# Scores on sixteen 32x32 tiles: x turned by VectorE in blocks, fixed PSUM banks, one x buffer

## The chip, the cores and the metric

One core of one Trainium2 chip. The metric is the device time in microseconds (us); the median of several executions is quoted. TensorE (PE in the profile) multiplies matrices into PSUM, a memory of eight banks of 128 x 512 fp32. VectorE (DVE), ScalarE (ACT) and GpSimd (POOL) work element by element, SyncE (SP) issues most DMA transfers. Ratios are the mean time of one kernel's fast runs over that of the other's fast runs of the same rounds, so they are not quite the ratio of the medians quoted.

## The reference

Eight batches of tokens (512 tokens, 8 heads of 64) attend to 32 state vectors per head, and the states attend to the tokens. A feed-forward layer with ELU follows.

```python
B, H, S, Ns, D = (8, 8, 512, 32, 64)
scores  = scale * x @ state.T          # softmax over the 32 states
xread   = softmax(scores) @ state
scores2 = scale * state @ x.T          # softmax over the 512 tokens
sread   = softmax(scores2) @ x
# rows of both, 8 x 544 tokens of 512, go through
h = rows @ w_in                        # 512 -> 2048
g = where(h > 0, h, exp(min(h, 0)) - 1)
out = g @ w_out                        # 2048 -> 512
```

x and state are random with a deviation of 0.1. Scores are therefore around 0.01, the softmax is nearly even, and a mistake in the scores hardly shows in the output.

## The kernel before

Both softmaxes come from one product, scores with states on partitions and tokens along the row. For it TensorE turns x, ACT copies the turned x out of PSUM, and TensorE multiplies on eight 64x32 tiles. `banks` hands out the one two-bank tile that all these steps share.

```python
xpool = pool("x", 2)
ps_a = pool("ps_a", 1, space=PSUM)     # 2 banks: turns, scores, m, state read
ps_h = pool("ps_h", 3, space=PSUM)     # hidden layer
ps_o = pool("ps_o", 3, space=PSUM)     # outputs

def turn_x(b, i):                      # 8 turns of 128x128; called twice a batch
    ps = banks([P, 2, R, P], "xT_ps")
    for j in range(2):
        for r in range(R):
            m = 2 * i + j
            transpose(ps[:, j, r], x_t[b][:, r, m * P : (m + 1) * P])

def by_state(b, name, rhs):            # scores, and m = states x w_in
    ps = banks([P, G, 512], name)
    for m in range(NP):
        for g in range(G):
            d = slice(g * D, (g + 1) * D)
            matmul(ps[m * NS : (m + 1) * NS, g], kT[d, b, m * NS : (m + 1) * NS],
                   rhs[m][d], start=True, stop=True, tile_position=(g * D, m * NS))
    return ps
# ... softmaxes on VectorE, ACT and GpSimd; state read; m ...
def ffn1(b, fo):                       # one of 16 parts of the hidden layer
    ps = ps_h.tile([P, S], FP32, tag="h", name="h_ps")
# ...
steps = [lambda i=i: (turn_x(b, i), copy_x(b, i)) for i in range(2)]
return steps + [s0, nop, nop, s1, lambda: (state_read(b), keep_read(b))]
```

After each hidden layer come two halves of a second product by Strassen's scheme (`p1` to `p7`: seven products of 16 instructions each, 3.46 us). The attention of the next batch is cut into the steps of the last line, and one step goes behind each product. In the first batch the order is a fixed plan, mixed with the conversion of the weights from fp64.

Of the kernel before, what the change touches and what calls it, by code (L numbers as in the profile page):

```python
# [10 lines left out]
FP32 = mybir.dt.float32  # L11
# [14 lines left out]
def kernel(  # L26
# [17 lines left out]
    DM, DF = moe_w_in.shape  # L44
    P = 128
    R = S // P
    NP = H // 2
    G = 2
    FO = DF // P
# [16 lines left out]
        return ctx.enter_context(tc.tile_pool(name=name, bufs=bufs, **kw))  # L66

    cpool = pool("const", 1)
    xpool = pool("x", 2)
    apool = pool("attn", 2)  # L70
    atpool = pool("aT", 4)
    mpool = pool("m", 2)
    work = pool("work", NRAW + 4)
    small = pool("small", 4)
    epool = pool("elu", 3)
    opool = pool("o", 2)
    ps_a = pool("ps_a", 1, space=PSUM)
    ps_h = pool("ps_h", 3, space=PSUM)
    ps_o = pool("ps_o", 3, space=PSUM)

    def banks(shape, name):
        return ps_a.tile(shape, FP32, tag="a", name=name)



# [48 lines left out]
        return raw  # L134

    def turn_states(raw):
        ps = st["k_ps"] = banks([P, B, P], "k_ps")
        for b in range(B):
            transpose(ps[:, b], raw[:, b].rearrange("p c d -> p (c d)"))

# [52 lines left out]

    def turn_x(b, i):

        ps = banks([P, 2, R, P], "xT_ps")
        for j in range(2):
            for r in range(R):
                m = 2 * i + j
                transpose(ps[:, j, r], x_t[b][:, r, m * P : (m + 1) * P])  # L200
        st[b, "xT", i] = ps
# [6 lines left out]
                out=xT[:, j], in_=st[b, "xT", i][:, j].rearrange("p r q -> p (r q)")  # L208
            )

    def by_state(b, name, rhs):


        ps = banks([P, G, 512], name)
        for m in range(NP):
            for g in range(G):
                d = slice(g * D, (g + 1) * D)
                matmul(
                    ps[m * NS : (m + 1) * NS, g],
                    kT[d, b, m * NS : (m + 1) * NS],  # L220
                    rhs[m][d],
                    start=True,
                    stop=True,
                    tile_position=(g * D, m * NS),
                )
        return ps

    def scores(b):

        st[b, "s_ps"] = by_state(b, "s_ps", [st[b, m] for m in range(NP)])  # L230



    def column_max(b, g):
        st[b, g, "top"] = top = small.tile([P, 1], FP32, name="top")
        vector.reduce_max(top, st[b, "s_ps"][:, g], axis=AX_X)
        vector.tensor_scalar(
            out=top, in0=top, scalar1=-scale, scalar2=None, op0=ALU.mult
        )

    def turn_scores(b, g):
        st[b, g, "t"] = t = apool.tile([P, NB, NS], FP32, name="t_sb")
        vector.transpose(t.rearrange("p k n -> p (k n)"), st[b, "s_ps"][:, g])

    def column_exp(b, g):
        st[b, g, "total"] = small.tile([P, 1], FP32, name="total")
        st[b, g, "a_s"] = apool.tile([P, S], FP32, name="a_s")
        scalar.activation(
            out=st[b, g, "a_s"], in_=st[b, "s_ps"][:, g], func=AF.Exp, scale=scale,
            bias=st[b, g, "top"], accum_out=st[b, g, "total"],  # L250
        )

# [33 lines left out]
        vector.transpose(st[b, g, "aT"], st[b, g, "t"].rearrange("p k n -> p (k n)"))  # L286

    def turn_state(b):
        ps = st[b, "sT"] = banks([P, G, R, P], "sT_ps")
        for g in range(G):  # L290
            a = st[b, g, "a_s"].rearrange("p (r q) -> p r q", r=R)
            for r in range(R):
                transpose(ps[:, g, r], a[:, r])
# [6 lines left out]
    def state_read(b):  # L300


        ps = st[b, "sr"] = banks([P, G, 512], "sr_ps")
        for g in range(G):
            for r in range(R):
                for m in range(NP):
                    matmul(
                        ps[m * NS : (m + 1) * NS, g, :D],
                        st[b, "aT_s"][:, g, r, m * NS : (m + 1) * NS],
                        x_t[b][:, r, m * P + g * D : m * P + (g + 1) * D],  # L310
                        start=(r == 0),
                        stop=(r == R - 1),
                        tile_position=(0, m * NS),
                    )
# [7 lines left out]

    def turn_read():

        ps = banks([P, B, NP, NS], "rT_ps")
        for b in range(B):
            transpose(ps[:, b].rearrange("p m s -> p (m s)"), read[:, b].rearrange("p g d -> p (g d)"))
        st["xT"] = work.tile([P, NP, B, NS], FP32, tag="w", name="xT_state")
        for e, k in ((scalar.copy, 0), (vector.tensor_copy, B // 2)):
            e(  # L330
                out=st["xT"][:, :, k : k + B // 2],
                in_=ps[:, k : k + B // 2].rearrange("p b m s -> p m b s"),
            )

    def make_m(b, c):

        cols = slice(c * 512, (c + 1) * 512)
        st[b, "m", c] = by_state(b, "m_ps", [w_in[:, m, cols] for m in range(NP)])

    def copy_m(b, c, engines):  # L340
        m_t[b, c] = mpool.tile([P, G, 512], FP32, name="m_sb")
# [22 lines left out]

    def ffn1(b, fo):

        ps = ps_h.tile([P, S], FP32, tag="h", name="h_ps")
        for k in range(G):
            matmul(
                ps,  # L370
                m_t[b, fo // 4][:, k, fo % 4 * P : (fo % 4 + 1) * P],
                st[b, k, "aT"],
                start=(k == 0),
                stop=(k == G - 1),
            )
        return ps

    def ffn1_state(fo):

        ps = ps_h.tile([P, B * NS], FP32, tag="h", name="h_ps")  # L380
        for co in range(NP):
            matmul(
                ps,
# [7 lines left out]
    def ffn2_row(ps, fo):  # L391
        for c in range(R):
# [4 lines left out]
                start=(fo == 0),  # L397
                stop=(fo == FO - 1),
            )

    def o_bank():
        return ps_o.tile([P, DM], FP32, tag="o", name="o_ps")


    w_k = w_out.rearrange("p (k e) (h q) -> p k e h q", e=2, h=2)
# [19 lines left out]
    class Strassen:  # L425
# [4 lines left out]


        def __init__(self, s):
            a = g_all.rearrange("p (k e) (s h q) -> p k e s h q", e=2, h=2, q=P)
            (self.a11, self.a21), (self.a12, self.a22) = (
                [a[:, :, e, s, h] for h in range(2)] for e in range(2)
            )
            self.o_sb = opool.tile([P, 2, DM], FP32, name="o_sb")
# [30 lines left out]

        def steps(self):
            t = lambda i: lambda k: t_w[i][k // (FO // 4)][:, k % (FO // 4)]  # L470
            ps = self.ps = {}

            def p1():
                ps["a"] = o_bank()
                self.product(ps["a"], self.a11, lambda k: b11[:, k], first=True)
                self.copy(ps["a"], 0, 0)

            def p2():
                ps["b"] = o_bank()
                self.product(ps["b"], self.a12, lambda k: b21[:, k], first=True, last=True)  # L480
                self.add(ps["b"], 0, 0)
                vector.tensor_tensor(
                    out=self.a12, in0=self.a12, in1=self.s2, op=ALU.subtract
                )

            def p6():
                self.product(ps["a"], self.s2, t(2))
                self.copy(ps["a"], 1, 0)

            def p7():  # L490
                ps["b"] = o_bank()
                self.product(ps["b"], self.a21, t(3), first=True)
                self.copy(ps["b"], 1, 1)

            def p5():
                self.product(ps["a"], self.s1, t(1))
                self.add(ps["a"], 1, 1)

            def p4():
                self.product(ps["b"], self.a22, t(4), last=True)  # L500
                self.add(ps["b"], 1, 0)

            def p3():
                self.product(ps["a"], self.a12, lambda k: b22[:, k], last=True)
                self.copy(ps["a"], 0, 1)

            return [p1, p2, p6, p7, p5, p4, p3]

    def attention(b):
# [5 lines left out]
                    f(b, g)  # L515

        def s0():
            scores(b)
            both(column_max, turn_scores, column_exp, row_max, row_subtract, row_exp)
            both(row_sum, row_scale, column_total)  # L520

# [3 lines left out]
            both(turn_tokens)  # L525

        nop = lambda: None
        steps = [lambda i=i: (turn_x(b, i), copy_x(b, i)) for i in range(2)]
        return steps + [s0, nop, nop, s1, lambda: (state_read(b), keep_read(b))]

    def store(b, i, o_sb):
        rows = out_b[b, 0:S].rearrange("(p r) c -> p r c", r=R)
        sync.dma_start(out=rows[:, 2 * i : 2 * i + 2], in_=o_sb)

    def first_batch():
# [19 lines left out]
            tt:1.1 sr:1 O:15 src:1 M:1.0  # L555
        """.split()
        make_identity(nc, ident)
        o_ps = [o_bank() for c in range(3)]
        o_ps += [ps_h.tile([P, DM], FP32, tag="h", name="o_ps")]
        order = [lambda n=n: load_w_in(0, n) for n in range(NP)]  # L560
        for c in range(1, FC + 1):
            if c < FC:
# [2 lines left out]
        w, h, e = [], {}, {}  # L565

        def fetch():
            if len(w) == 28:
                load_x(1, [sync])
            if len(w) < len(order):  # L570
                w.append(order[len(w)]())

# [54 lines left out]
    def batch(b):  # L627
        for fo in range(FO):
            elu(ffn1(b, fo), fo)
            if fo % 4 == 1 and fo // 4 + 1 < FC:  # L630
                full_m(b, fo // 4 + 1)
        nxt = b + 1 < B
        hooks = attention(b + 1) if nxt else []
        if b + 2 < B:
            hooks += [lambda: load_x(b + 2, [sync])]
        two = [Strassen(i) for i in range(2)]
        two[0].sums()
        for i in range(2):
# [22 lines left out]

    first_batch()
    load_x(2, [sync])
    for e in (vector, scalar, gpsimd):
        e.on = False
    for i in (1, 2, 4, 3):
# [34 lines left out]
```

## Time and profile before

| | before |
|---|---|
| time, median | 797.78 us |
| span of the profiled execution | 795.6 us |
| TensorE busy | 756.3 us, 95% |
| VectorE, ACT busy | 43%, 40% |
| one batch, 2 and later | 85.75 us, TensorE without a gap |
| of it: two turns of x, scores | 2 x 0.87 us, 1.02 us |

Read it from the chain of work that ended last. It is followed back from the last instruction; a share of 93% on TensorE means that almost nothing but TensorE's own work stands between the start and the end. Its lines are in the prediction.

### The profile page before, as it was taken

The numbers are of one execution on the slowest core, as the hardware profiler recorded it, in microseconds if no ns is written. First come the engines' busy times: TensorE is split into PE (matmuls) and PEld (weight loads), VectorE is DVE, ScalarE is ACT, GpSimd is POOL, SyncE is SP. The second block draws the span as 40 slices with busy tenths as digits, with TensorE's granted clock in tenths as the row PEclk, the third lists the DMA queues.
The fourth block names the chain that finished last, engine by engine and source line by source line (L and its number), as shares of the span: only waits on it lengthen the run. The fifth ranks groups of instructions, "written<-read, shape, count | busy, mean of one in ns | idle before, by whom it ended". The sixth has DMA issues, their size and how long they took to land.

```text
span 795.6 us, 9330 instructions
## 1 busy us (share of the span) xinstructions
PE 756.3 (95%) x3808; PEld 500.9 (63%) x3808; DVE 343.4 (43%) x577; ACT 320.7 (40%) x596; POOL 34.1 (4%) x38
## 2 busy tenths in 40 slices
PE   2389999999999999999999999999999999999996
PEld 1034454358863887368845885488647884588885
DVE  1899958546024721464135612472146313511140
ACT  2889853562136311642055213631264206400420
POOL 0100002002000010002000200010000200000000
PEclk9979999999999999999999999999999999999999
DMA  9757200400300030001100030003000000000001
GB/s 220 276 158 222 103 1 1 106 1 1 80 27 0 2 80 27 1 0 45 37 26 1 1 80 27 0 1 80 27 0 1 29 0 27 1 26 1 28 0 27
DMA packets 42795, 35.21 MB, mean 44 GB/s; under 512 B 36352, under 2 KB 36352, under 8 KB 42752
## 3 DMA queue, kind: packets, MB, share of 16 engines
q1 hardware_dynamic: 38592, 33.56, 14.6%
q10 hardware_dynamic: 4160, 1.05, 0.7%
q8 instruction: 30, 0.49, 0.3%
q14 instruction: 13, 0.11, 0.0%
HBM read 25.69 MB, written 8.91 MB: 43 GB/s over the span
## 4 chain that ended last, share of the span: by engine, by line
PE 93%; DVE 4%; DMA 1%; ACT 0%; issue 0%; ACTq 0%
PE o_ps L92 52%; PE h_ps L92 32%; PE m_ps L92 4%; PE xT_ps L92 2%; DVE w_in L92 1%; PE s_ps L92 1%; DMA x_sb<-in_x_dram 1%; DVE t_w L92 1%; PE sr_ps L92 1%; PE sT_ps L92 1%; DVE total_t L92 1%; DMA s_sb<-in_state_dram 0%; DVE w_out L92 0%; ACT xT L92 0%; PE k_ps L92 0%; DVE aT L92 0%
## 5 line engine op out<-in xcount | busy, mean ns | idle before, releaser
L92 PE MATMUL o_ps<-w_out,g_all 128*128 128x256 f32 (+1 forms) x1088 | 274.8, 406 | 0.0
L92 PEld LDWEIGHTS o_ps<-w_out,g_all 128*128 128x128 f32 x1088 | 204.2, 190 | 62.8 <-issue 35.8
L92 PE MATMUL h_ps<-aT,m_sb 128*128 128x512 f32 x512 | 232.1, 603 | 9.4 <-DVE aT L92 7.9
L92 PEld LDWEIGHTS h_ps<-aT,m_sb 128*128 128x128 f32 x512 | 96.1, 192 | 139.5 <-issue 112.2
L92 DVE SCALAR_TENSOR_TENSOR g_all<-e_sb,h_ps 128x512 f32<-128x512 f32 (+1 forms) x144 | 94.5, 657 | 193.8 <-ACT e_sb L92 193.8
L92 ACT ACTIVATE e_sb<-h_ps 128x512 f32<-128x512 f32 (+1 forms) x144 | 82.4, 572 | 96.3 <-PE h_ps L92 96.2
L92 ACT COPY o_sb<-o_ps 128x256 f32<-128x256 f32 (+1 forms) x62 | 23.3, 378 | 240.2 <-PE o_ps L92 240.2
L92 PE MATMUL o_ps<-t_w,s 128*128 128x256 f32 x480 | 109.1, 380 | 0.0
L92 PEld LDWEIGHTS o_ps<-t_w,s 128*128 128x128 f32 x480 | 90.2, 190 | 16.8 <-ACT o_sb L92 5.0
L92 ACT ACTIVATE e_sb<-e_sb 128x512 f32<-128x512 f32 (+1 forms) x144 | 87.2, 606 | 4.5
L92 DVE TENSOR_TENSOR o_sb<-o_sb,o_ps 128x256 f32<-128x256 f32 x45 | 18.6, 414 | 158.1 <-issue 82.8
L92 PE MATMUL o_ps<-t_w,g_all 128*128 128x256 f32 x240 | 54.2, 379 | 0.0
L92 PEld LDWEIGHTS o_ps<-t_w,g_all 128*128 128x128 f32 x240 | 45.6, 190 | 6.2
L92 PE MATMUL m_ps<-w_in,kT 64*32 64x512 f32 x512 | 37.6, 615 | 6.9 <-ACT a_s L92 6.9
L92 ACT ACTIVATE raw<-raw 128x512 f32<-128x512 uint32 x64 | 43.6, 681 | 1.0
L92 POOL TENSOR_TENSOR t_sb<-t_sb,top_t 128x512 f32<-128x512 f32 x16 | 16.9, 1061 | 573.0 <-DVE top_t L92 560.3
L92 DVE COPY m_sb<-m_ps 128x512 f32<-128x512 f32 x28 | 19.2, 685 | 42.0 <-ACT m_sb L92 42.0
L92 ACT COPY xT<-xT_ps 128x512 f32<-128x512 f32 x32 | 17.2, 589 | 35.0 <-PE xT_ps L92 35.0
L92 PE MATMUL h_ps<-xT_state,w_in 128*128 128x256 f32 x128 | 27.8, 379 | 0.0
L92 PEld LDWEIGHTS h_ps<-xT_state,w_in 128*128 128x128 f32 x128 | 24.3, 190 | 3.3
L92 PEld LDWEIGHTS m_ps<-w_in,kT 64*32 64x32 f32 x512 | 6.0, 105 | 31.3 <-issue 20.9
L92 ACT COPY m_sb<-m_ps 128x512 f32<-128x512 f32 x36 | 20.3, 576 | 8.5 <-PE m_ps L92 8.5
(54 smaller groups left out, 388.2 us busy)
## 6 DMA issues: line engine op xcount, KB each, us to landing
raw<-in_moe_w_in_dram SPq DMA_DIRECT2D x16, 512.0 KB, 5.0
raw<-in_moe_w_out_dram SPq DMA_DIRECT2D x16, 512.0 KB, 4.9
out_dram<-o_sb SPq DMA_DIRECT2D x16, 512.0 KB, 2.7
x_sb<-in_x_dram SPq DMA_DIRECT2D x28, 256.0 KB, 4.9
x_sb<-in_x_dram ACTq DMA_DIRECT2D x4, 256.0 KB, 6.9
s_sb<-in_state_dram SPq DMA_DIRECT2D x8, 64.0 KB, 5.1
out_dram<-o_sb SPq DMA_DIRECT2D x8, 64.0 KB, 1.7
```

The lines of the kernel that those rows point to most:

```text
L92: ins = getattr(self.engine, name)(*args, **kw)
```

## The change

Its intent is to take the turns of x off TensorE. VectorE turns 32x32 blocks (point 4 of the prediction's list), so the scores become products of 32x32 blocks: sixteen tiles at once, four row tiles of tokens (`a`) by four column tiles of heads (`m`), each row tile writing to a bank of its own. VectorE also turns the states into blocks. PSUM becomes one fixed tile with banks by number, and x has one buffer because the turned blocks need the space of the other.

```diff
-    xpool = pool("x", 2)
+    xpool = pool("x", 1)
+    xbpool = pool("xb", 1)
-    ps_a = pool("ps_a", 1, space=PSUM)
-    ps_h = pool("ps_h", 3, space=PSUM)
-    ps_o = pool("ps_o", 3, space=PSUM)
+    psum = pool("ps", 1, space=PSUM).tile([P, 8, 512], FP32, name="ps")
...
+    def turn_blocks(b):
+        st[b, "xb"] = xbpool.tile([P, R, DM], FP32, name="xb")
+        for r in range(R):
+            vector.transpose(st[b, "xb"][:, r], x_t[b][:, r])
...
+    def block_scores(b):
+        for g in range(G):
+            for i in range(D // 32):
+                for m in range(NP):
+                    k = (2 * m + g) * (D // 32) + i
+                    for a in range(4):
+                        rows = slice(a * 32, (a + 1) * 32)
+                        matmul(
+                            psum[m * NS : (m + 1) * NS, 4 + a, g * P : (g + 1) * P],
+                            st[b, "kb"][rows, k],
+                            st[b, "xb"][rows, :, k * 32 : (k + 1) * 32].rearrange("p r j -> p j r"),
+                            start=(i == 0), stop=(i == D // 32 - 1),
+                            tile_position=(a * 32, m * NS),
+                        )
...
     def ffn1(b, fo):
-        ps = ps_h.tile([P, S], FP32, tag="h", name="h_ps")
+        ps = bank(4 + fo % 2 if b == 0 else 3 + fo % 3)
...
-            if len(w) == 28:
-                load_x(1, [sync])
+            if len(w) == len(order):
+                if 1 not in x_t:
+                    load_x(1, [sync])
...
-        steps = [lambda i=i: (turn_x(b, i), copy_x(b, i)) for i in range(2)]
-        return steps + [s0, nop, nop, s1, lambda: (state_read(b), keep_read(b))]
+        return [nop, s0, nop, nop, s1, lambda: (state_read(b), keep_read(b))]
```

Partition p of x holds tokens 4p to 4p+3 (index r). `rearrange("p r j -> p j r")` makes the columns of a product come out in token order, at the price of an innermost step of 512 floats, 2 KB. Batches 0 and 1 keep the old way. Left out of the cut: the states are loaded four times, one under the other, for their turn, and the outputs of batches 2 to 7 are stored in the new order of tokens.

More of the change, by code (lines that the diff above doesn't have):

```diff
@@ L46 @@
     R = S // P
+    TURNED = 2
     NP = H // 2
@@ L73 @@
     work = pool("work", NRAW + 4)
+    reppool = pool("rep", 1)
     small = pool("small", 4)
@@ L76, with bank, pair @@
     opool = pool("o", 2)
-    ps_a = pool("ps_a", 1, space=PSUM)
-    ps_h = pool("ps_h", 3, space=PSUM)
-    ps_o = pool("ps_o", 3, space=PSUM)
-    def banks(shape, name):
-        return ps_a.tile(shape, FP32, tag="a", name=name)
+    psum = pool("ps", 1, space=PSUM).tile([P, 8, 512], FP32, name="ps")
+    def bank(i):
+        return psum[:, i]
+    def pair(pattern, i=6, **sizes):
+        flat = psum[:, i : i + 2].rearrange("p b q -> p (b q)")
+        return flat.rearrange("p " + pattern, **sizes)
     class InOrder:
@@ L136, in turn_states @@
     def turn_states(raw):
-        ps = st["k_ps"] = banks([P, B, P], "k_ps")
+        ps = st["k_ps"] = pair("(b q) -> p b q", q=P)
         for b in range(B):
@@ L194, in turn_x @@
     def turn_x(b, i):
-        ps = banks([P, 2, R, P], "xT_ps")
+        ps = pair("(j r q) -> p j r q", j=2, q=P)
         for j in range(2):
@@ L209, in copy_x, with load_rep, by_state @@
             )
-    def by_state(b, name, rhs):
-        ps = banks([P, G, 512], name)
+    def load_rep(b):
+        st[b, "rep"] = reppool.tile([P, H, D], FP32, name="rep")
+        for a in range(4):
+            sync.dma_start(
+                out=st[b, "rep"][a * NS : (a + 1) * NS], in_=state[b].rearrange("h n d -> n h d")
+            )
[3 more added lines that the diff above has]
+            vector.transpose(st[b, "xb"][:, r], x_t[b][:, r])
+        st[b, "kb"] = reppool.tile([P, 2 * H, NS], FP32, name="kb")
+        vector.transpose(
+            st[b, "kb"].rearrange("p k n -> p (k n)"),
+            st[b, "rep"].rearrange("p h d -> p (h d)"),
+        )
+    def block_scores(b):
[3 more added lines that the diff above has]
+                    k = (2 * m + g) * (D // 32) + i
+                    for a in range(4):
+                        rows = slice(a * 32, (a + 1) * 32)
[3 more added lines that the diff above has]
+                            st[b, "xb"][rows, :, k * 32 : (k + 1) * 32].rearrange("p r j -> p j r"),
+                            start=(i == 0),
+                            stop=(i == D // 32 - 1),
+                            tile_position=(a * 32, m * NS),
+                        )
+        st[b, "s_ps"] = [psum[:, 4:8, g * P : (g + 1) * P] for g in range(G)]
+    def by_state(b, rhs):
+        ps = psum[:, 6:8]
         for m in range(NP):
@@ L228, in scores @@
     def scores(b):
-        st[b, "s_ps"] = by_state(b, "s_ps", [st[b, m] for m in range(NP)])
+        ps = by_state(b, [st[b, m] for m in range(NP)])
+        st[b, "s_ps"] = [ps[:, g] for g in range(G)]
     def column_max(b, g):
         st[b, g, "top"] = top = small.tile([P, 1], FP32, name="top")
-        vector.reduce_max(top, st[b, "s_ps"][:, g], axis=AX_X)
+        ps = st[b, "s_ps"][g]
+        axes = mybir.AxisListType.X if len(ps.shape) == 2 else mybir.AxisListType.XY
+        vector.reduce_max(top, ps, axis=axes)
         vector.tensor_scalar(
@@ L242, in turn_scores @@
         st[b, g, "t"] = t = apool.tile([P, NB, NS], FP32, name="t_sb")
-        vector.transpose(t.rearrange("p k n -> p (k n)"), st[b, "s_ps"][:, g])
+        ps = st[b, "s_ps"][g]
+        if len(ps.shape) == 2:
+            vector.transpose(t.rearrange("p k n -> p (k n)"), ps)
+        else:
+            vector.transpose(t.rearrange("p (a k) n -> p a (k n)", a=4), ps)
     def column_exp(b, g):
@@ L247, in column_exp @@
         st[b, g, "a_s"] = apool.tile([P, S], FP32, name="a_s")
+        a_s, ps = st[b, g, "a_s"], st[b, "s_ps"][g]
+        if len(ps.shape) == 3:
+            a_s = a_s.rearrange("p (r a j) -> p a j r", r=R, a=4)
+            ps = ps.rearrange("p a (j r) -> p a j r", r=R)
         scalar.activation(
-            out=st[b, g, "a_s"], in_=st[b, "s_ps"][:, g], func=AF.Exp, scale=scale,
+            out=a_s, in_=ps, func=AF.Exp, scale=scale,
             bias=st[b, g, "top"], accum_out=st[b, g, "total"],
@@ L288, in turn_state @@
     def turn_state(b):
-        ps = st[b, "sT"] = banks([P, G, R, P], "sT_ps")
+        ps = st[b, "sT"] = pair("(g r q) -> p g r q", g=G, q=P)
         for g in range(G):
@@ L300, in state_read @@
     def state_read(b):
-        ps = st[b, "sr"] = banks([P, G, 512], "sr_ps")
+        ps = st[b, "sr"] = psum[:, 6:8]
         for g in range(G):
@@ L323, in turn_read @@
     def turn_read():
-        ps = banks([P, B, NP, NS], "rT_ps")
+        ps = pair("(b m s) -> p b m s", b=B, s=NS)
         for b in range(B):
@@ L337, in make_m @@
         cols = slice(c * 512, (c + 1) * 512)
-        st[b, "m", c] = by_state(b, "m_ps", [w_in[:, m, cols] for m in range(NP)])
+        st[b, "m", c] = by_state(b, [w_in[:, m, cols] for m in range(NP)])
     def copy_m(b, c, engines):
@@ L378, in ffn1_state @@
     def ffn1_state(fo):
-        ps = ps_h.tile([P, B * NS], FP32, tag="h", name="h_ps")
+        ps = bank(3 + fo % 3)[:, : B * NS]
         for co in range(NP):
@@ L399, in ffn2_row @@
             )
-    def o_bank():
-        return ps_o.tile([P, DM], FP32, tag="o", name="o_ps")
     w_k = w_out.rearrange("p (k e) (h q) -> p k e h q", e=2, h=2)
@@ L432, in __init__ @@
         def __init__(self, s):
+            self.banks = bank(2 * s), bank(1)
             a = g_all.rearrange("p (k e) (s h q) -> p k e s h q", e=2, h=2, q=P)
@@ L470, in steps @@
             t = lambda i: lambda k: t_w[i][k // (FO // 4)][:, k % (FO // 4)]
-            ps = self.ps = {}
+            bank_a, bank_b = self.banks
             def p1():
-                ps["a"] = o_bank()
-                self.product(ps["a"], self.a11, lambda k: b11[:, k], first=True)
-                self.copy(ps["a"], 0, 0)
+                self.product(bank_a, self.a11, lambda k: b11[:, k], first=True)
+                self.copy(bank_a, 0, 0)
             def p2():
-                ps["b"] = o_bank()
-                self.product(ps["b"], self.a12, lambda k: b21[:, k], first=True, last=True)
-                self.add(ps["b"], 0, 0)
+                self.product(bank_b, self.a12, lambda k: b21[:, k], first=True, last=True)
+                self.add(bank_b, 0, 0)
                 vector.tensor_tensor(
@@ L486, in p6 @@
             def p6():
-                self.product(ps["a"], self.s2, t(2))
-                self.copy(ps["a"], 1, 0)
+                self.product(bank_a, self.s2, t(2))
+                self.copy(bank_a, 1, 0)
             def p7():
-                ps["b"] = o_bank()
-                self.product(ps["b"], self.a21, t(3), first=True)
-                self.copy(ps["b"], 1, 1)
+                self.product(bank_b, self.a21, t(3), first=True)
+                self.copy(bank_b, 1, 1)
             def p5():
-                self.product(ps["a"], self.s1, t(1))
-                self.add(ps["a"], 1, 1)
+                self.product(bank_a, self.s1, t(1))
+                self.add(bank_a, 1, 1)
             def p4():
-                self.product(ps["b"], self.a22, t(4), last=True)
-                self.add(ps["b"], 1, 0)
+                self.product(bank_b, self.a22, t(4), last=True)
+                self.add(bank_b, 1, 0)
             def p3():
-                self.product(ps["a"], self.a12, lambda k: b22[:, k], last=True)
-                self.copy(ps["a"], 0, 1)
+                self.product(bank_a, self.a12, lambda k: b22[:, k], last=True)
+                self.copy(bank_a, 0, 1)
             return [p1, p2, p6, p7, p5, p4, p3]
@@ L517, in s0 @@
         def s0():
-            scores(b)
+            block_scores(b)
             both(column_max, turn_scores, column_exp, row_max, row_subtract, row_exp)
@@ L527, in attention @@
         nop = lambda: None
-        steps = [lambda i=i: (turn_x(b, i), copy_x(b, i)) for i in range(2)]
-        return steps + [s0, nop, nop, s1, lambda: (state_read(b), keep_read(b))]
+        return [nop, s0, nop, nop, s1, lambda: (state_read(b), keep_read(b))]
     def store(b, i, o_sb):
-        rows = out_b[b, 0:S].rearrange("(p r) c -> p r c", r=R)
+        if b < TURNED:
+            rows = out_b[b, 0:S].rearrange("(p r) c -> p r c", r=R)
+        else:
+            rows = out_b[b, 0:S].rearrange("(r p) c -> p r c", r=R)
         sync.dma_start(out=rows[:, 2 * i : 2 * i + 2], in_=o_sb)
@@ L557, in first_batch @@
         make_identity(nc, ident)
-        o_ps = [o_bank() for c in range(3)]
-        o_ps += [ps_h.tile([P, DM], FP32, tag="h", name="o_ps")]
+        o_ps = [bank(c) for c in range(R)]
         order = [lambda n=n: load_w_in(0, n) for n in range(NP)]
@@ L631, in batch @@
                 full_m(b, fo // 4 + 1)
+            if fo == 8 and b + 1 < B:
+                turn_blocks(b + 1)
         nxt = b + 1 < B
@@ L634, in batch @@
         if b + 2 < B:
-            hooks += [lambda: load_x(b + 2, [sync])]
+            hooks += [lambda: (load_x(b + 2, [sync]), load_rep(b + 2))]
         two = [Strassen(i) for i in range(2)]
@@ L663 @@
     load_x(2, [sync])
+    load_rep(2)
     for e in (vector, scalar, gpsimd):
```

## The prediction

> **What bounds the kernel now.** I read the page's engine shares first, then the chain of work that ended last, then one stretch of that chain in order of time, and last the groups of instructions, each shape apart. The first two say that TensorE is the bound and nothing else is near it:
>
> ```profile
> PE 756.3 (95%) x3808; PEld 500.9 (63%) x3808; DVE 343.4 (43%) x577; ACT 320.7 (40%) x596; POOL 34.1 (4%) x38
> ...
> PE 93%; DVE 4%; DMA 1%; ACT 0%; issue 0%; ACTq 0%
> ```
>
> From batch 2 on, the chain is TensorE without a gap. This is its second-product stage in one batch, start, duration, what; the same piece returns every 85.75 us (173.84, 259.60, 345.35):
>
> ```profile
> 259.60 3.45 PE o_ps L92 x16
> 263.05 0.87 PE xT_ps L92 x8
> 263.92 3.46 PE o_ps L92 x16
> 267.38 0.87 PE xT_ps L92 x8
> 268.25 3.46 PE o_ps L92 x16
> 271.71 1.02 PE s_ps L92 x16
> 272.73 10.56 PE o_ps L92 x48
> 283.29 0.87 PE sT_ps L92 x8
> 284.16 3.46 PE o_ps L92 x16
> 287.61 1.03 PE sr_ps L92 x64
> ```
>
> See that the two turns of x (xT_ps) lie on the path at their full 0.87 us each, and the scores (s_ps) at 1.02. Whatever TensorE is spared here comes off the end; whatever VectorE gains here costs nothing unless TensorE has to wait for it. VectorE's unit of work is this (mean ns of one at the end):
>
> ```profile
> L92 DVE STREAM_TRANSPOSE t_sb<-s_ps 128x512 f32<-128x512 f32 x16 | 11.1, 702 | 0.0
> L92 DVE STREAM_TRANSPOSE aT<-t_sb 128x512 f32<-128x512 f32 x16 | 11.2, 704 | 18.0 <-POOL t_sb L92 18.0
> ```
>
> **What the Trainium skill says.** (1) TensorEngine Tiling (Array Packing), Key Properties: a change of tiling mode drains TensorE, and different tiles run in parallel. The trace agrees: scores are 16 instructions of 512 columns on 64x32 tiles, eight at once; from the second product's rate (3.455 us for 16 of 256 columns, 0.84 ns a column) two rounds of eight take 0.86 us, and 1.02 was measured, so about 0.16 us goes to entering and leaving the mode. (2) TensorE: Matmul & The Clock Gate, The mechanism (Part 3): concurrent tiles start about 4 ns apart. In this trace's single instructions they start 6.7 ns apart (s_ps, and sr_ps in bursts of four every 56 ns); I use 6.7. (3) SBUF — State Buffer, Door 1 (the note on cachelines): reads that stay in a 16-byte line run at full rate, each access to another line is penalised. No run so far shows it: every moving operand before is contiguous over at least 64 elements. (4) VectorE: DVE Perf Modes, The three transpose paths: VectorE turns only 32x32 blocks; the trace has 0.70 us for 128x512, from PSUM or SBUF.
>
> **The change part by part.**
>
> Removed from TensorE: two turns in each of batches 2 to 7, 12 x 0.87 = 10.4 us, all on the path. ACT also loses their copies, off the path.
>
> Exchanged on TensorE: the scores. Now 64 matmuls per batch, 128 instructions (this trace has two per fp32 matmul), each of 128 columns on one of sixteen tiles. At 0.84 ns a column one takes about 107 ns; sixteen issue in 16 x 6.7 = 107 ns, so issue just keeps up. 128/16 = 8 rounds x 107 = 0.86 us, plus 0.16 to 0.2 for the mode: 1.05 us, the same as now. But its moving operand is read in the order (j, r), the innermost step being 512 floats: each of its 128 columns lies in another line than the one before. If that halves the rate, it is 8 x 214 + 0.2 = 1.9 us, 0.9 more in each of six batches, 5.4 us in all. I can't decide between these from the trace and take half, 2.7 us.
>
> Added to VectorE: five turns of 128x512 a batch, 5 x 0.70 = 3.5 us. The order of the built program puts the four of x not in the first product, where they are written, but into the second half of the batch before, right behind the adds of the fifth and fourth products, and that of the state behind the second product's add. VectorE serves in order, so they may hold it until x has landed. State read ends; x then loads in some 7 us (below); turns done by about 7.5 us after. The next add that TensorE needs comes with the end of the third product after the state read (10.4 us), and is needed 3.5 us later. So hidden, with some 3 us to spare. The second half's sums now also stand ahead of the second product's add and of the score reductions: VectorE reaches the maxima about 2.5 us after the scores are done instead of at once. Counted along before's chain (maximum at 187.14 to second aT at 198.47, 11.3 us) the add of the fifth product is done about 1 to 2 us before the third product (p3) needs its bank. Hidden, but narrowly.
>
> One x buffer: from batch 2 on harmless, as above. In the first batch it isn't. x of batch 1 was loaded at 72 us; now its load waits until the state read of batch 0 has freed the buffer, and TensorE wants it one product later:
>
> ```profile
> 110.96 1.10 PE L92 MATMUL sr_ps<-x_sb,aT_s 128*32 128x64 f32 x64
> 111.99 3.70 PE L92 MATMUL o_ps<-w_out,g_all 128*128 128x512 f32 x8
> 115.52 1.04 PE L92 MATMUL xT_ps<-ident,x_sb 128*128 128x128 f32 x8
> ```
>
> A load of x that starts at 202.8 moves data until about 210 (in the table of 2 us stretches its DMA share is 0.96 for 208 to 210 and 0.03 after), with a store of 512 KB just ahead of it. Without that, some 7 us: 112.1 + 7 = 119.1 against 115.6. Stall 3.5 us (2.5 to 5), all on the path.
>
> Fixed banks: before, the first matmul of batch 1 took whichever h bank was free. Now it is bank 3, which holds the fourth output of batch 0, and VectorE empties that bank last:
>
> ```profile
> 141.41 1.12 PE L92 MATMUL h_ps<-aT,m_sb 128*128 128x512 f32 x2 [0.75 <-ACT m_sb L92]
> 142.59 0.68 DVE L92 COPY m_sb<-m_ps 128x512 f32<-128x512 f32 x1
> 143.19 1.27 DVE L92 COPY o_sb<-o_ps 128x512 f32<-128x512 f32 x2
> 143.32 2.84 PE L92 MATMUL h_ps<-aT,m_sb 128*128 128x512 f32 x6 [0.79 <-DVE m_sb L92]
> ```
>
> The first matmul would start at 144.5, not 141.4, and 0.86 us of work that filled the wait for m_sb comes after it: 144.5 - 143.3 + 0.86 = 2.1 us lost, once. The built program agrees: that matmul now waits for VectorE and ACT at once, and the second, which waited for VectorE, waits for nothing. Against this, waits by region instead of by whole tile let the second turn of x(0) start after one copy instead of two at the start: perhaps 0.5 us gained.
>
> Sum: 797.7 - 10.4 + 2.7 + 3.5 + 2.1 - 0.5 = 795.1; with a little for waits I haven't seen, 795.5.
>
> **The rivals.** *Strided reads cost much more than half the rate.* Four times: 8 x 428 = 3.6 us a batch, 2.6 more than now, 15.6 in all: 808. For: two streams[...] and sixteen tiles read at once. Against: before's state read also feeds four streams to each partition at full rate. *They cost nothing*: 792 to 793. *VectorE becomes the bound locally*: if p3 or the next second product waits a microsecond in each of six batches, 6 us more, 801. For: VectorE's queue is in order and its slack at p3 is 1 to 2 us; exp into the token order (r, a, j) also writes with a stride. Against: VectorE is 43% busy and gains only 6 x 3.5 = 21 us. *The stalls of the first batch don't come*, as x lands early or the idle time is made up: 790. Against: TensorE is at 20.00 busy of 20 us in each stretch from 60 to 120 us, so nothing makes it up.
>
> **Range and chances.** The terms I know leave 792 to 793, the stride adds 0 to 6 with even chances, a repeated wait 0 to 6 with less. I give 790.5 to 803. Faster by over 2% (under 781.8) would need more than the whole 10.4 us plus another 5: 1%. Slower by over 2% (over 813.7) needs the worst stride and the repeated wait together: 3%.
>
> **What would show it.** Chain of a late batch: no xT_ps, scores of 1.05 (no penalty) or 1.9 us (half rate), period 84.0 or 84.9 instead of 85.75, and no piece of VectorE between. TensorE idle some 3.5 us at about 115 us, put down to the load of x; its first product of batch 1 idle until VectorE's last o_sb copy. Turns of x on VectorE of 0.70 us each. I am wrong if scores take over 2.5 us, if idle time of TensorE returns in every batch with VectorE as releaser, or if the first batch shows no idle time before x of batch 1 is turned.

## The result

The time is **803.53 us** (803.09 to 804.36, four runs) against 797.78 us before: ratio 1.0074, interval 1.0056 to 1.0091. It is slower, by less than 1%, but clear of the noise, and lies just above the predicted range. The profiled execution was the slowest of the four: its span is 802.6 us, 7.0 more than the 795.6 of before.

The shares and the chain of the page of the changed kernel:

```profile
PE 759.4 (95%) x4384; PEld 502.3 (63%) x4384; DVE 363.4 (45%) x607; ACT 312.6 (39%) x572; POOL 34.1 (4%) x38
...
PE 88%; DVE 7%; DMA 3%; ACT 1%; issue 0%; SPq 0%; ACTq 0%; DVEq 0%
```

TensorE is still the bound, and it is *not* less busy: 759.4 us, with 576 instructions more. The turns are gone, and something has taken their place. The share of the chain that is not TensorE's grew from 7% to 12%: there are new waits as well. A steady stretch, engine by engine in order of time (start, duration, instruction, and in brackets the idle time before it and what ended that), shows the first:

```profile
188.18 2.77 PE L100 MATMUL ps<-xb,kb 32*32 32x128 f32 x128
189.32 0.41 DVE L100 TENSOR_TENSOR o_sb<-o_sb,ps 128x256 f32<-128x256 f32 x1
...
190.88 3.72 PE L100 MATMUL ps<-t_w,s 128*128 128x256 f32 x16
...
206.93 4.21 SPq L100 DMA_DIRECT2D x_sb<-in_x_dram  x4
...
210.09 0.71 DVE L100 STREAM_TRANSPOSE xb<-x_sb 128x512 f32<-128x512 f32 x1 [3.80 <-DMA x_sb<-in_x_dram]
...
214.66 0.71 DVE L100 STREAM_TRANSPOSE xb<-x_sb 128x512 f32<-128x512 f32 x1 [0.67 <-DMA x_sb<-in_x_dram]
...
217.53 0.42 DVE L100 TENSOR_TENSOR o_sb<-o_sb,ps 128x256 f32<-128x256 f32 x1 [2.15 <-PE ps L100]
```

The scores take 190.88 - 188.18 = 2.70 us of TensorE's time; before it was 1.02. The prediction had named over 2.5 us as a sign that it is wrong. The next batch's scores start at 273.86, so the period is 85.68 us, where 84.0 or 84.9 was predicted. VectorE does stand waiting for x for 3.8 us with its queue blocked, as predicted, and nobody minds: its next add comes in time, at 217.53.

The chain through the end of the first batch (start, duration, what) shows the other two places:

```profile
99.62 11.75 PE ps L100 x108
...
113.50 4.53 DMA x_sb<-in_x_dram
...
118.07 12.87 PE ps L100 x49
...
146.35 0.60 DVE m_sb L100
146.96 1.21 DVE o_sb L100 x2
148.30 151.77 PE ps L100 x966
```

At 113.5 the end of the kernel hangs on the load of x of batch 1. At 146.96 it hangs on VectorE's copies of batch 0's outputs. From 148.30 on it is TensorE without a gap.

Four milestones place the 7.0 us:

| milestone on TensorE | before | after | shift | added since |
|---|---|---|---|---|
| state read of batch 0 starts | 110.96 | 110.23 | -0.73 | -0.73 |
| second turn of x of batch 1 starts | 118.12 | 121.81 | +3.69 | +4.42 |
| second m of batch 1 starts, after eight matmuls of the hidden layer | 146.09 | 153.59 | +7.50 | +3.81 |
| end of the span | 795.6 | 802.6 | +7.0 | -0.5 |

So six batches together gave only 0.5 us: 12 x 0.87 = 10.4 us of turns saved, 6 x (2.70 - 1.02) = 10.1 us of scores paid. And two places that run once cost 8.2 us. About 3 us of these are no waiting at all (e8 below splits them), as TensorE's own lines at the second place show:

```profile
148.30 5.36 PE L100 MATMUL ps<-aT,m_sb 128*128 128x512 f32 x8 [3.95 <-DVE o_sb L100]
153.59 1.09 PE L100 MATMUL ps<-w_in,kT 64*32 64x512 f32 x16
```

After idling 3.95 us, eight matmuls take 153.59 - 148.30 = 5.29 us to the next start. The same eight take 3.52 us in batch 2 of the kernel before (228.32 to 231.84). The table of short stretches says why; its columns are stretch and length, busy time of PE, PEld, DVE, ACT and POOL, then the granted clock of TensorE, DMA share and GB/s:

```profile
118.00:120.00 2.00, 1.93 (x6) 1.46 (x7) 0.00 (x0) 1.15 (x2) 0.00 (x0) 0.50 0.00 0
120.00:122.00 2.00, 2.00 (x6) 0.91 (x5) 0.00 (x0) 0.02 (x1) 0.00 (x0) 0.75 0.03 8
148.00:150.00 2.00, 1.70 (x2) 0.84 (x3) 0.15 (x1) 0.00 (x0) 0.00 (x0) 0.57 0.78 313
150.00:152.00 2.00, 2.00 (x4) 0.86 (x3) 0.00 (x0) 0.02 (x1) 0.00 (x0) 0.57 0.97 231
```

The granted clock is 0.50 to 0.75 right behind each of the two waits; it was 1.00 from 110 to 114 and from 143 to 148 us. Each slow stretch lasts some 3.4 us (0.54 on average from 117.3 to 120.8 us, 0.53 from 148.1 to 151.6). The Trainium skill, TensorE: Matmul & The Clock Gate, What's actually happening (Part 1), says that the clock halves after an idle window of about 3.4 us, and that the window runs free of what the kernel does. The trace agrees at the second place, where TensorE idled for 3.95 us. At the first it idled for 0.81, 0.87 and 0.59 us with single turns of x between, and the clock fell all the same.

### The profile page after: what moved, and what is told of

It is laid out like the page before. It is cut to its first block, busy times and chain, and to the rows that moved or that the text cites. A ratio compares the mean times of both kernels' runs of the same rounds, so it can differ in the third digit from the quotient of the medians.

```text
span 802.6 us, 10525 instructions
## 1 busy us (share of the span) xinstructions
PE 759.4 (95%) x4384; PEld 502.3 (63%) x4384; DVE 363.4 (45%) x607; ACT 312.6 (39%) x572; POOL 34.1 (4%) x38
## 3 DMA queue, kind: packets, MB, share of 16 engines
q10 hardware_dynamic: 4160, 1.05, 0.8%
## 4 chain that ended last, share of the span: by engine, by line
PE 88%; DVE 7%; DMA 3%; ACT 1%; issue 0%; SPq 0%; ACTq 0%; DVEq 0%
PE ps L100 88%; DVE w_in L100 2%; DMA x_sb<-in_x_dram 2%; DVE w_out L100 1%; DVE t_w L100 1%; DMA raw<-in_moe_w_in_dram 1%; DVE total_t L100 1%; DMA raw<-in_moe_w_out_dram 0%; ACT e_sb L100 0%; DVE g_all L100 0%; ACT raw L100 0%; SPq L100 0%; DVE aT L100 0%; DVE top L100 0%; DVE kT L100 0%
## 5 line engine op out<-in xcount | busy, mean ns | idle before, releaser
L100 PE MATMUL ps<-w_out,g_all 128*128 128x256 f32 (+1 forms) x1088 | 272.2, 405 | 0.2 <-DVE w_out L100 0.2
L100 PE MATMUL ps<-aT,m_sb 128*128 128x512 f32 x512 | 233.4, 606 | 12.2 <-DVE aT L100 7.9
L100 PEld LDWEIGHTS ps<-w_out,g_all 128*128 128x128 f32 x1088 | 205.7, 190 | 59.0 <-issue 30.3
L100 PEld LDWEIGHTS ps<-aT,m_sb 128*128 128x128 f32 x512 | 96.7, 193 | 143.0 <-issue 117.4
L100 DVE SCALAR_TENSOR_TENSOR g_all<-e_sb,ps 128x512 f32<-128x512 f32 (+1 forms) x144 | 94.6, 657 | 198.9 <-ACT e_sb L100 198.9
L100 ACT ACTIVATE e_sb<-ps 128x512 f32<-128x512 f32 (+1 forms) x144 | 82.5, 573 | 102.4 <-PE ps L100 102.3
L100 PE MATMUL ps<-t_w,s 128*128 128x256 f32 x480 | 109.8, 382 | 0.0
L100 PEld LDWEIGHTS ps<-t_w,s 128*128 128x128 f32 x480 | 90.2, 190 | 19.2 <-ACT o_sb L100 5.0
L100 PE MATMUL ps<-t_w,g_all 128*128 128x256 f32 x240 | 54.3, 379 | 0.0
L100 PEld LDWEIGHTS ps<-t_w,g_all 128*128 128x128 f32 x240 | 45.2, 190 | 5.9
```

What stands on the lines that cost most here:

```text
L100: ins = getattr(self.engine, name)(*args, **kw)
```

## The experiments

My theory after the result had four parts: the strided read halves the rate of the scores; something in the supply of small instructions costs about as much again; the load of x and the choice of the bank each stop TensorE once; and each stop is followed by a stretch at half clock. The rivals were that sixteen tiles are slow in themselves, that the stops are made up later, and that the slow matmuls after the stops have another cause. Nine kernels were run; their expectations are quoted as they stood before. They were run at other times.

The comparison with the reference passed for all nine, also for the two that are wrong (e4, e9), for the reason given with the reference. So the values were also computed in simulation with x and state ten times larger: the changed kernel, e1 and e5 then agree with the reference to a relative error of 4e-6 (norm of the difference over norm of the output), and e4 and e9 are off by 1.1 and 0.8.

### e1: contiguous reads

x of batches 2 to 7 is loaded with token r*128 + p at partition p. Then a row of 32 columns is contiguous for every r, and only the reader of the scores permutes.

```diff
-        x_v = x[b].rearrange("h (p r) d -> p r h d", r=R)
+        order = "h (p r) d -> p r h d" if b < TURNED else "h (r p) d -> p r h d"
+        x_v = x[b].rearrange(order, r=R)
...
-   st[b, "xb"][rows, :, k * 32 : (k + 1) * 32].rearrange("p r j -> p j r"),
+   st[b, "xb"][rows, :, k * 32 : (k + 1) * 32],
...
+   t.rearrange("p (r a) n -> p r a n", a=4), ps.rearrange("p a (r n) -> p r a n", r=R)
...
-            a_s = a_s.rearrange("p (r a j) -> p a j r", r=R, a=4)
-            ps = ps.rearrange("p a (j r) -> p a j r", r=R)
+            a_s = a_s.rearrange("p (r a j) -> p r a j", r=R, a=4)
+            ps = ps.rearrange("p a (r j) -> p r a j", r=R)
```

> The changed kernel with one difference: x of batches 2 to 7 is loaded so that the scores' moving operand is read in runs of 32 contiguous elements instead of one element every 2 KB; exp then also writes in order. The scores take 2.70 us per batch now. Stride theory: the strided read is what makes them slow, so they fall to 1.05 to 1.3 us, exp from 1.15 to about 0.7 us, the time by 6 x 1.5 = 9 us to about 794.5. Rival, supply: after the first 32 pairs the trace shows pairs of weight load and matmul coming 16.7 ns apart, so 128 pairs can't take less than about 1.8 to 2.2 us whatever the stride: time about 799. Second rival, sixteen tiles into four banks are slow in themselves: still 2.7 us and 803.5 us.

Measured: 798.75 us (797.91 to 800.63), ratio to before 1.0017 (1.0005 to 1.003). The groups of the scores and of exp in the changed kernel, busy time and mean ns of one after the bar:

```profile
L100 PE MATMUL ps<-xb,kb 32*32 32x128 f32 x768 | 16.5, 390 | 0.0
L100 ACT ACTIVATE a_s<-ps,top 128x512 f32<-128x512 f32 x16 | 16.6, 1041 | 53.1 <-DVE top L100 48.9 <-DVE t_sb L100 4.2
```

and in e1:

```profile
L100 PE MATMUL ps<-xb,kb 32*32 32x128 f32 x768 | 11.4, 278 | 0.0
L100 ACT ACTIVATE a_s<-ps,top 128x512 f32<-128x512 f32 x16 | 11.0, 688 | 53.1 <-DVE top L100 48.9 <-DVE t_sb L100 4.2
```

From start to the next product's start the scores now take 189.52 - 187.69 = 1.83 us. The stride was 2.70 - 1.83 = 0.87 us of each batch, 5.2 us in six; the time fell by 4.8. Exp, which wrote with the same disorder, fell from 1.15 us in batch 2 to a mean of 0.69, off the path. But 1.83 is not the 1.02 of before: the stride theory alone fails, and so does "sixteen tiles are slow in themselves", which had the scores stay at 2.7 us. The supply rival's 1.8 to 2.2 is what came.

### e2: x of batch 1 early

Two x buffers no longer fit. But the buffer of the turned blocks is idle until batch 2's blocks are turned, so x of batch 1 is loaded there, at its old place in the order.

```diff
-        x_t[b] = xpool.tile([P, R, DM], FP32, name="x_sb")
+        if b == 1:
+            x_t[b] = xbpool.tile([P, R, DM], FP32, tag="xb", name="x_sb")
+        else:
+            x_t[b] = xpool.tile([P, R, DM], FP32, name="x_sb")
...
-            if len(w) == len(order):
-                if 1 not in x_t:
-                    load_x(1, [sync])
+            if len(w) == 28:
+                load_x(1, [sync])
```

> The changed kernel with x of batch 1 loaded early, as in the kernel before, into the buffer that later holds the turned blocks (two x buffers don't fit). Theory: the wait at about 115 us (3.5 us) goes, and with it the stretch at half the granted clock right after it (0.9 us): about 799.1 us, clock 1.00 from 110 to 125 us. Rival, the wait only but no clock loss: 800.0. Rival, the wait was made up later: 803.5, with the idle time back at the start of batch 1.

Measured: 799.44 us (798.67 to 800.07), 4.1 less than the changed kernel. The granted clock from 110 to 126 us is 1.00 throughout, and the piece of DMA is gone from the chain. The wait at the start of batch 1 stays (first matmul at 142.93 us), with a granted clock of 0.50 behind it. The time doesn't separate 799.1 from the 800.0 of the rival without a loss of clock; TensorE's own lines do. From the state read of batch 0 to the second turn of x of batch 1 it takes 116.43 - 109.27 = 7.16 us, as before the change (118.12 - 110.96), against 11.58 in the changed kernel. Both the wait and its aftermath were on the path, and nothing made them up.

### e3: another bank first

```diff
-        ps = bank(4 + fo % 2 if b == 0 else 3 + fo % 3)
+        ps = bank(4 + fo % 2 if b == 0 else 3 + (fo + 1) % 3)
```

> The changed kernel with the hidden layer's banks of batches 1 to 7 rotated by one, so that the first matmul of batch 1 doesn't go into the bank that VectorE empties last. Theory: the lost 2.1 us of waiting return, and since TensorE isn't idle for 3.9 us there is no stretch at a granted clock of 0.57 after it (1.9 us more): about 799.5 us. Rival, the clock has nothing to do with that wait: 801.4. Rival, another wait takes its place (m of batch 1 from VectorE): 803.

Measured: 799.60 us (798.65 to 801.12), 3.9 less. In its table of stretches the granted clock is 1.00 from 138 to 150 us. TensorE still waits for m of batch 1 in two pieces of some 0.75 us, as before the change; that is all. From the second turn of x to the second m of batch 1 it takes 148.66 - 120.67 = 27.99 us, against 27.97 before and 31.78 in the changed kernel: the waiting and the slow clock of the second place both come from the choice of one bank. One thing was not expected: behind the wait for x, which this kernel still has, the clock was 1.00 in this execution, where the changed kernel had 0.50. Up to there the two programs are the same, so whether this wait slows the clock is a matter of the execution, and the medians mix both cases.

### e4: the stride alone, on eight tiles

The kernel before, with the scores' moving operand read in another order (so the scores belong to other tokens).

```diff
-        st[b, "s_ps"] = by_state(b, "s_ps", [st[b, m] for m in range(NP)])
+        turned = [st[b, m].rearrange("p (r q) -> p q r", r=R) for m in range(NP)]
+        st[b, "s_ps"] = by_state(b, "s_ps", turned)
```

> The kernel before with one difference that makes the result wrong on purpose: the scores, on eight 64x32 tiles with 512 columns, read their moving operand with an innermost step of 128 elements. Stride theory: half rate, so the scores take 0.16 + 2 x 0.86 = 1.9 us instead of 1.02, 0.86 x 8 batches = 6.9 us more, about 804.5 us. If a step over several lines costs more than half the rate: 2.7 us and more, 811. Rival, strided reads cost nothing and the sixteen tiles are slow in themselves: 1.02 us and 797.8 us.

Measured: 806.00 us (805.93 to 806.02), 8.4 more than before (797.63 in the same rounds). In order of time:

```profile
187.66 2.33 PE L92 MATMUL s_ps<-xT,kT 64*32 64x512 f32 x16
189.91 2.43 PE L92 MATMUL o_ps<-w_out,g_all 128*128 128x256 f32 x10
```

The scores take 2.25 us here instead of 1.02, and 2.05 to 2.25 in the batches from 2 on. Without the 0.16 of changing the mode that is 1.9 to 2.1 for columns that took 0.86, so here the stride costs a factor of 2.2 to 2.4, somewhat more than the 2 I expected. It needs no sixteen tiles: the rival that a stride costs nothing falls.

### e5: the three cures together

The edits of e1, e2 and e3 in one kernel.

> The three cures together: contiguous reads of the scores, x of batch 1 loaded early, banks rotated. Theory: their gains add, since each removes time from TensorE's own path in another place: 803.5 - 4.8 - 4.1 - 3.9 = 790.7 us, no idle time of TensorE above 1 us after 60 us, period of a batch about 84.9 us. Rival, a wait of VectorE that they uncover (the fifth product's add, or m of batch 1) takes part of it: 793 or more.

Measured: 791.00 us (790.00 to 791.13), ratio to before 0.9915 (0.9901 to 0.9928): 0.85% faster than the kernel before, 1.6% faster than the changed one. The sum of the three gains, 790.7, is met. The chain after the first batch is one piece of TensorE:

```profile
141.57 168.61 PE ps L100 x1049
```

So no wait of VectorE was uncovered, and the three costs were independent. This is the version that beats both kernels.

### e6: the tiles in another order

As e5, with the loops over `m` and `a` exchanged.

```diff
-                for m in range(NP):
-                    k = (2 * m + g) * (D // 32) + i
-                    for a in range(4):
-                        rows = slice(a * 32, (a + 1) * 32)
+                for a in range(4):
+                    rows = slice(a * 32, (a + 1) * 32)
+                    for m in range(NP):
+                        k = (2 * m + g) * (D // 32) + i
```

> As the three cures together, but the sixteen tiles are gone through with the column tile innermost instead of the row tile. The scores with contiguous reads took 1.9 us per batch, not the 1.05 that issue and columns allow. If it is the order of the tiles that makes the pairs come 16.7 ns apart and wait between groups of sixteen, they change by more than 0.2 us per batch: down to 1.1 us, 786 us. If it is the supply of instructions, which doesn't know the order: 1.9 us per batch and the same time as with the row tile innermost, within 0.5 us.

Measured: 790.97 us (790.36 to 791.60), and the scores busy 11.4 us as in e5. The order makes no difference.

### e7: one x buffer, in the kernel before

```diff
-    xpool = pool("x", 2)
+    xpool = pool("x", 1)
...
-            if len(w) == 28:
-                load_x(1, [sync])
+            if len(w) == len(order):
+                if 1 not in x_t:
+                    load_x(1, [sync])
```

> The kernel before with one x buffer instead of two and nothing else. Theory: TensorE waits 3.5 us for x of batch 1 at about 115 us, and [...]it also runs about 1.8 us at half clock: 797.6 + 3.5 to 4.4 = about 801.5 us. Later batches, which load x right after the state read of the batch before and turn it 60 us later, lose nothing. Rival, the later batches lose as well: 803 or more. Rival, the wait is hidden in this kernel: 797.6.

Measured: 802.17 us (802.02 to 802.74), 4.4 more than before (797.75 in the same rounds). TensorE waits three times for a piece of x, 0.59, 0.87 and 0.68 us, with single turns between. The stretch behind it:

```profile
120.00:122.00 2.00, 2.00 (x3) 0.68 (x2) 0.00 (x0) 0.93 (x2) 0.00 (x0) 0.50 0.00 0
```

Four matmuls that take 1.72 us before take 3.19 here. The later batches have the pieces and the period of before. So this part of the change costs 4.4 us by itself, all in the first batch. The clock fell although TensorE was never idle for a microsecond at a stretch; the lone turns between the waits did not keep it up.

### e8: the waits filled with work

The changed kernel with seven matmuls into free banks, of constants, read by nobody.

```diff
+    def fill(i, n):
+        for _ in range(n):
+            matmul(bank(i), ident, w_in[:, 0, :512], start=True, stop=True)
...
+                if num == [1, 0]:
+                    fill(5, 3)          # before x of batch 1 is turned
...
+        if b == 1:
+            fill(4, 4)                  # before the first matmul of batch 1
```

> The changed kernel with seven matmuls added whose results nobody reads: three of 0.85 us while TensorE waits for x of batch 1, four while it waits for its first bank in batch 1. They take the idleness away and leave both waits. Theory, idleness lowers the granted clock afterwards: although work is added, the time falls by up to 2.8 us, to about 801, the granted clock is 1.00 at 118 to 122 and at 148 to 152 us, and the eight matmuls after the second wait take 3.5 instead of 5.4 us. Rival, those matmuls were slow for another reason (the operands being written meanwhile by the load of x or the copies): no change, 803.5, or up to 0.5 us more.

Measured: 801.39 us (799.96 to 801.68): 2.1 less than the changed kernel, with work added. In order of time, and the stretches that showed 0.57 before:

```profile
146.97 3.67 PE L100 MATMUL ps<-aT,m_sb 128*128 128x512 f32 x8 [0.32 <-DVE o_sb L100]
150.57 1.09 PE L100 MATMUL ps<-w_in,kT 64*32 64x512 f32 x16
```

```profile
148.00:150.00 2.00, 2.00 (x6) 0.85 (x5) 0.00 (x0) 1.01 (x2) 0.00 (x0) 1.00 1.06 317
150.00:152.00 2.00, 2.00 (x19) 0.48 (x18) 0.69 (x1) 1.51 (x4) 0.00 (x0) 1.00 1.05 229
```

The wait still ends with VectorE's copy, but the eight matmuls take 150.57 - 146.97 = 3.60 us instead of 5.29, at full clock. Idleness was the cause of the slow stretch, and not the loads and copies that run at that time. As the waits stay and the clock doesn't fall, this run splits the milestones.

```profile
110.16 1.10 PE L100 MATMUL ps<-x_sb,aT_s 128*32 128x64 f32 x64
...
120.47 1.04 PE L100 MATMUL ps<-ident,x_sb 128*128 128x128 f32 x8
```

From the state read of batch 0 to the second turn of x it takes 120.47 - 110.16 = 10.31 us (7.16 before, 11.58 in the changed kernel, and 10.20 in e3's execution with its clock of 1.00): 3.1 us are the wait, 1.3 the clock. From there to the second m of batch 1 it takes 150.57 - 120.47 = 30.10 us (27.97 and 31.78): 2.1 us are the wait, 1.7 the clock.

### e9: half as many score instructions

As e5, with 32 matmuls of 256 columns instead of 64 of 128 (wrong).

```diff
-            for i in range(D // 32):
+            for i in range(1):
...
-   psum[m * NS : (m + 1) * NS, 4 + a, g * P : (g + 1) * P],
+   psum[m * NS : (m + 1) * NS, 4 + a, 2 * g * P : 2 * (g + 1) * P],
...
-   st[b, "xb"][rows, :, k * 32 : (k + 1) * 32],
+   st[b, "xb"][rows, :, k * 32 : (k + 2) * 32],
...
-                            stop=(i == D // 32 - 1),
+                            stop=True,
```

> The three cures together, but the scores as half as many matmuls of twice the columns (32 of 256 instead of 64 of 128, the same 0.86 us of columns for sixteen tiles; the scores are wrong on purpose). Supply theory: what holds the scores at 1.85 us is the number of instructions, so half as many take 1.05 to 1.25 us, 6 x 0.7 = 4 us less than the 791.0 of the three cures: about 787. Rival, sixteen tiles at once can't be fed with columns faster: still 1.8 us, 791.

Measured: 788.12 us (787.46 to 788.84), 2.9 less than e5. In order of time:

```profile
180.23 1.49 PE L100 MATMUL ps<-xb,kb 32*32 32x256 f32 x64
181.66 3.72 PE L100 MATMUL ps<-t_w,s 128*128 128x256 f32 x16
```

The scores take 1.43 us, between the two expectations. That fits one simple account, with one constant for three kernels. Call a pass one round over the sixteen tiles with both instructions of each fp32 matmul. e5 has four passes, e9 two, and both have 0.86 us of columns and 0.16 us of mode changes. What is left is 1.83 - 1.02 = 0.81 for four passes and 1.43 - 1.02 = 0.41 for two: **0.2 us a pass**. The changed kernel fits too: 0.16, plus 2 x 0.86 for strided columns, plus 4 x 0.2, is 2.68, and 2.70 was measured. (The 0.16 is taken over from eight tiles.) In the single instructions the first pass starts its pairs 6.7 ns apart, and the later ones some 16.7 ns apart with a hole before the second tile; from pass to pass e5 takes 0.43 us, of which 0.22 are columns. Not every pass over tiles costs that: the state read before, 16 rounds of 64 columns on four tiles, takes 1.03 us, which is its columns (16 x 54 ns) and the 0.16. Whether the supply of instructions makes the 0.2, or a dependency at the first tile of a pass, these runs don't tell; only that the order of tiles doesn't matter, and that the number of instructions, or of passes, which e9 halves with it, does.

## Why the prediction was wrong

By its own steps, against the profiled execution:

- **Removed turns, 10.4 us:** right. They are gone from the chain and nothing of their length took their place as waiting.
- **Scores, "issue just keeps up":** this step failed. It took the 6.7 ns between tiles, measured in bursts of four and eight, as a rate that holds for 128 pairs in a row. Only the first pass starts at that rate, and on average a pass costs 0.2 us beyond its columns. Measured 1.83 us instead of 1.05 with contiguous reads (e1, e5), 4.7 us in six batches that the sum doesn't have.
- **Scores, strided read, "half" of 5.4 us:** the mechanism was right and the size wrong by the hedge. The full half rate holds: 0.87 us a batch, 5.2 us (e1 against the change), where the sum had 2.7. The cacheline note cited there gives no figure; these runs give a factor of 2 on 32x32 tiles and 2.2 to 2.4 on 64x32 (e4).
- **VectorE's added turns and the later maxima, "hidden, narrowly":** right. The chain of a batch holds TensorE only, and the turns took 0.71 us each. The last turn of x ended 8.6 us after the state read (7.5 predicted), and the maxima began 1.05 us after the scores (2.5 predicted).
- **One x buffer, 3.5 us:** the wait was right in place and cause, and 3.1 us in size (e8). Missing is the clock: 1.3 us, together the 4.4 us of the milestones, and 4.4 us again in e7.
- **Fixed banks, 2.1 us:** the wait was right, 2.1 us (e8). Missing again is the clock: 1.7 us; together 3.8 us in the milestones and 3.9 us in e3.
- **The start, 0.5 us gained:** 0.73 was. It was not taken apart further, and executions with the same program up to there (e1, e3, e8 and the changed kernel) start the state read anywhere from 109.81 to 110.47 us.

With the measured terms the sum is -10.4 + 10.1 + 4.4 + 3.8 - 0.7 = +7.2 us, against +7.0 between the two profiles. The medians differ by 5.75 us, since the profiled execution of the changed kernel was the slowest of its four. The largest misses are the passes (4.7), the clock (3.0) and the stride (2.5). The rival "strided reads cost much more than half the rate" was the right worry with the wrong reason: the scores landed between its 3.6 us and my 1.9, but more than half of the surprise wasn't the stride. The page on the clock was cited for the tiles, and its first part, which bears on every new wait, was not applied.

## What to carry to other kernels

When an engine that is the bound gets a new wait of a few microseconds, count the wait and then the stretch at lower clock behind it; useless work in the wait can even be cheaper than idleness. A short burst does not give the rate of a long one: price many small matmuls by passes over the tiles, from a pass measured on the same tiles, and keep the moving operand contiguous, if need be by changing the order of the load. And look at what a change does once, not only per batch: here two places that run once cost nearly as much as was saved in six batches, and curing them together with the stride turned 0.7% slower into 0.85% faster.

## What the Trainium skill lacked or had wrong

- SBUF — State Buffer, Door 1 (the note on cachelines): it has no size for TensorE's penalty. Measured: a moving operand with an innermost step of 2 KB streams at half rate on 32x32 tiles (2.70 against 1.83 us for the scores), with a step of 512 bytes on 64x32 tiles at 1/2.2 to 1/2.4 (2.05 to 2.25 against 1.02 us, 0.16 us of each being mode changes by the estimate above). ACT's exp writing with a step of 512 bytes took 1.15 us instead of 0.69.
- TensorE: Matmul & The Clock Gate, Part 3: its span of a pack, duration plus 4 ns for each further tile, is for a single pass. Measured: tiles start 6.7 ns apart in a first pass, and repeated passes of 32 instructions cost 0.2 us each beyond their columns (1.83 us for four, 1.43 for two).
- The same page, Part 1 (What's actually happening): right about the halved clock after idleness (0.50 to 0.57 here). Its example in HAM oscillation has DMA waits of some 3 to 5 us, each followed by 1.67 us of throttled work; it has no number for shorter waits with work between. Here the wait of 3.9 us cost 1.7 us more, and three waits of 0.59 to 0.87 us with lone turns between cost about 1.5 us more in e7; behind the same wait for x the clock was 0.50 in one kernel's profiled execution and 1.00 in another's.
